# Attention and a GeGLU feed-forward interleaved on one core: down products in one run of 48, gate and up banks read early, maxima of the lead placed earlier

## The chip, the cores and the metric

The kernel runs on one core of a Trainium2 chip. The metric is the device time of one execution in microseconds (us). A comparison of two kernels uses several runs of each; the profile is of one execution. The engines are called TensorE (PE, its weight loads PEld), VectorE (DVE), ScalarE (ACT), GpSimd (POOL) and SyncE (SP, which issues the transfers). L12 is line 12 of the kernel.

## What is computed

```python
xn = layernorm(x)                                  # x: 1 x 2048 x 576
q, k, v = split(xn @ wqkv)                         # 32 heads of 18
p = softmax(q @ k.T * 18 ** -0.5)                  # for each head, 2048 x 2048
s = (p @ v, heads side by side) @ wo
g = silu((gelu(xn @ w_gate) * (xn @ w_up)) @ w_down)   # 576 -> 4608 -> 576, gelu in its tanh form
out = x + s * g
```

All is float32. A factor of a product is split in two parts, high and low (`hi`, `lo`), and a product is made of three: high by high, low by high and high by low.

## The kernel before

A first part (to about 197 us) normalizes x, transposes it, and stores q and k (`qk`), v (`vs`) and the split x (`xhs`) in DRAM. The rest is one long sequence of **144 sections**, each made by `section()` (L422). TensorE runs in the order in which the program is written (`manual_schedule`, L71); on the other engines a scheduler places the instructions, except where `keep_in_program_order` is written.

The feed-forward works on 4 blocks of 512 tokens. A block has 36 sections, each with 128 of the 4608 hidden columns. A section makes 27 *pairs* (`gate_up`, L356): one matmul for gate (`pg`) on the lower 64 rows of the array and one for up (`pu`) on the upper 64, at the same time. Then `activate` (L376) makes gelu(gate) * up in `t1`: ScalarE squares pg (L379), VectorE makes a product with pg (L380), ScalarE takes a tanh (L381), VectorE makes a product with pg (L382) and one with pu (L383). `finish` (L454) splits `t1` into `hh` and `hl`, and after each second section (`G` = 2) it splits the rows of w_down into `dh` and `dl`. `down` (L386) multiplies them: for each of 4 token groups and 2 halves of the columns, 6 matmuls into a bank `py`, which VectorE adds to `Y` (L402; L400 copies in a block's first time). Two sections give 48 such matmuls. `finish` puts them on a list in two halves (24 each, L467 and L468), the first due in the next section and the second in the one after; `downs` (L450) takes from the list what is due.

Attention is woven into this. A *slot* is one part of keys for four heads; it needs maxima (`pm`, `max_mm` L626, read by VectorE at L635) and scores (`pe`, `score_mm` L653, read by ScalarE's exp at L662). Maxima run 40 slots ahead of scores. Sections 0 to 8 are the *lead*: they make maxima only, as many slots as `FIRST` (L41) says. Sections 9 to 136 have 8 slots each: in 16 more pairs a score takes one half of the array and a maximum the other. `spread` (L56) places these special pairs evenly among the 27. After its pairs a section makes the products with v (`values`, L687): 16 groups of matmuls with 32 columns of weights each, four side by side, into `acc` (the profile shows 32 rows for a section). Every fourth section transposes the maxima in between (`max_end`, L641; pm at L644). Sections 132 to 136 have scores only, and 137 to 143 no attention.

After the products with v come, where they are due, the output projection of an earlier block (`project_o`, L523, 15 matmuls into `po`; eight of them for a block, in eight sections one after the other, placed at L564 to L578), and then `downs`. So TensorE's order in a section is: 43 pairs, acc, (pm), (po), 24 py, and the pairs of the next section.

PSUM has 8 banks: tag `f` (2) for pg and pu, `m` (3) for pm and po, `s` (2) for pe and py, and one for acc. So the next section's first pair needs the banks of pg and pu that `activate` of this section reads. When a block is complete, `gates` (L408) takes silu of `Y` in eight pieces (a tanh at L416, two operations on POOL, a store to `ys`); four are done in each of two sections. Key loads (`load_k`, L590, 12 transfers each) and the loads of q (`load_q`, L614) go through SP's queue, as all loads.

The functions that the diff touches follow.

Of the kernel before, what the change touches and what calls it, by code (L numbers as in the profile page):

```python
# [38 lines left out]
NR = F // (G * P)  # L39
NF = NB * NR * G  # L40
FIRST = (0, 3, 5, 5, 5, 5, 5, 6, 6)  # L41
MROW = 3 * DH
HO = 7
KO = HO * DH
# [22 lines left out]
def kernel(ctx: ExitStack, tc: tile.TileContext, x, wqkv, wo, w_gate, w_up, w_down, out):  # L67
# [302 lines left out]

    def gate(o, th, yy):

        nc.scalar.activation(th, yy, AF.Tanh, scale=0.5)
        nc.vector.scalar_tensor_tensor(o, th, 1.0, yy, op0=ALU.add, op1=ALU.mult)

    def activate(pg, pu):  # L376
        t1 = ffn.tile([P, TB], F32, name="t1", bufs=1)
        t2 = ffn.tile([P, TB], F32, name="t2", bufs=1)
        nc.scalar.activation(t1, pg, AF.Square)  # L379
        nc.vector.scalar_tensor_tensor(t2, t1, 1.0 / GC, pg, op0=ALU.add, op1=ALU.mult)  # L380
        nc.scalar.activation(t1, t2, AF.Tanh, scale=GC * GS)  # L381
        nc.vector.scalar_tensor_tensor(t2, t1, 1.0, pg, op0=ALU.add, op1=ALU.mult)  # L382
        nc.vector.scalar_tensor_tensor(t1, t2, 0.5, pu, op0=ALU.mult, op1=ALU.mult)  # L383
        return t1

    def down(b, r, hs, wd, Y, js):  # L386
# [21 lines left out]
    def gates():  # L408

        for k, (b, j, c, Y) in enumerate(FF["gates"]):  # L410
            rows, cc = slice(b * TB + j * P, b * TB + (j + 1) * P), slice(288 * c, 288 * c + 288)
            if k < 3:
                th = op.tile([P, 288], F32, name="th", tag=("yy", "yy", "xx")[k], bufs=(2, 2, 1)[k])
            else:
                th = ffn.tile([P, 288], F32, name="th")
            tc.keep_in_program_order(nc.scalar.activation(th, Y[:, j, cc], AF.Tanh, scale=0.5))  # L416
            nc.gpsimd.tensor_scalar(th, th, 1.0, 1.0, op0=ALU.add, op1=ALU.mult)
            nc.gpsimd.tensor_tensor(th, th, Y[:, j, cc], op=ALU.mult)
            nc.sync.dma_start(ys[rows, cc], th)
        FF["gates"] = []  # L420

    def section(specials=(), tag="f", raw_d=None, early=None):  # L422

        n = FF["n"]
        FF["n"] += 1
        b, r = divmod(n // G, NR)
        g = n % G
        pairs, pg, pu = gate_up(tag)
        if g == 0:
            FF["hs"] = []  # L430
        keep = tc.keep_in_program_order if n == NU * NA + len(FIRST) + 1 else lambda i: i
        nxt = load_gu((n + 1) % (NR * G), keep) if n + 1 < NF else None
        if nxt:
            for k in range(NG - 1):
                split_gu(nxt, k)
        if g == G - 1:
            raw = FF["rawd"] = raw_d() if raw_d else raw_tile([P, G, D])
            nc.sync.dma_start(raw, w_down[r * G * P:(r + 1) * G * P, :].rearrange("(g p) n -> p g n", p=P))
            if early:
                FF["wd"] = early(raw)  # L440
        for p in spread(pairs, specials):
            p()
        if nxt:
            split_gu(nxt, NG - 1)
        FF["w"] = nxt
        if n + 1 < NF and (n + 1) % (NR * G) == 0:
            FF["xd"] = load_xd(b + 1)
        FF["act"] = activate(pg, pu)

    def downs():  # L450
        while FF["down"] and (FF["down"][0][-1] < FF["n"] or FF["n"] == NF):
            down(*FF["down"].pop(0)[:-1])

    def finish(pool=ffn, cut=split, bufs=1):  # L454

        n = FF["n"] - 1
        b, r = divmod(n // G, NR)
        hh = ffn.tile([P, TB], F32R, name="hh", bufs=G + 1)
        hl = ffn.tile([P, TB], F32R, name="hl", bufs=G + 1)
        cut(hh, hl, FF["act"])  # L460
        FF["hs"].append((hh, hl))
        if n % G == G - 1:
            wd = FF.pop("wd", None)
            if not wd:
                wd = [pool.tile([P, G, D], F32R, name=m, bufs=bufs) for m in ("dh", "dl")]
                cut(*wd, FF["rawd"])
            for h in range(2):  # L467
                FF["down"].append((b, r, FF["hs"], wd, FF["Y"], (2 * h, 2 * h + 1), n + 1 + h))  # L468


    op = ctx.enter_context(tc.tile_pool(name="op", bufs=1, reuse_waits="tile"))
# [51 lines left out]
    def project_o(b, i, S2=None, o=None):  # L523
        c, j = divmod(i, TB // P)
        cc = place(b, i)[1]
        if b < NB - 1:
            xx, yy = OG["xy"]
        po = ps.tile([P, TB], F32, name="po", tag="m", bufs=3)
        o = o or OG["o"]
        terms = [(k, x, w) for k in range(NK) for x, w in ((0, 0), (0, 1), (1, 0))]  # L530
        for m, (k, x, w) in enumerate(terms):
            n = min(KO, D - k * KO)
            nc.tensor.matmul(po[:, 0:288], o[x][0:n, k, :], OW[w][0:n, k, :], start=(m == 0), stop=(m == len(terms) - 1))  # L533
        if b < NB - 1:
            nc.vector.scalar_tensor_tensor(yy, yy, 0.5, po[:, 0:288], op0=ALU.mult, op1=ALU.mult)
            nc.gpsimd.tensor_tensor(yy, yy, xx, op=ALU.add)
            OG["y", b, i] = yy
        elif S2 is not None:
            nc.scalar.activation(S2[:, j, cc], po[:, 0:288], AF.Copy)
        return po[:, 0:288]  # L540
# [16 lines left out]
    for b in range(NB):  # L557
        last = b == NB - 1
        for k in range(NK):
            t0 = b * AB + max(-(-min(H, (k + 1) * HO) // QD) * NA + 3, 2 * NA + 10 + 3 * k)  # L560
            if not (last and k == NK - 1):
                at(t0, 0, load_o, b, k)
                at(t0 + 2 - last, 2, norm_o, k)
        first = (b + 1) * AB + 1 if last else max((b + 1) * AB + 6, (b + 1) * NR * G - len(FIRST) + 3)  # L564
        at(first - 2, 0, load_wo, 0)
        at(first - 1, 2, split_o, 0)
        for i in range(GROUPS):
            n = first + i
            if last and n >= ENDS - 1:
                continue  # L570
            if not last:
                at(n, 0, load_xy, b, i)
                at(n + 1, 0, store_y, b, i)
            at(n, 1, lambda b=b, i=i: project_o(b, i, S2[0]))
            if i == TB // P - 1:
                at(n + 1, 0, load_wo, 1)
            if i + 1 < GROUPS:
                at(n, 2, split_o, i + 1)  # L578


    with tc.tile_pool(name="att", bufs=1, reuse_waits="tile") as att:
# [5 lines left out]
        for vv in VS:  # L587
            nc.vector.memset(vv[:, VC * VW:], 0.0)

        def load_k(n, keep=lambda i: i):  # L590

            u, c = divmod(n, NA)
            if u >= NU:
                return
            cols = slice(c * TB, (c + 1) * TB)
            for r in range(2):
                for a in range(2):
                    kk = f(KS[n % KB][r])[64 * a:64 * a + MROW, :]
                    h = QD * (u % NQ) + 2 * r + a
                    rows = slice(D + h * DH, D + (h + 1) * DH)  # L600
                    for n_, i in enumerate((0, 1, 0)):
                        keep(nc.sync.dma_start(kk[n_ * DH:(n_ + 1) * DH, :], qk[i, rows, cols]))
# [8 lines left out]

        QS, MX, ACC, PT, NM, DEN = {}, {}, {}, {}, {}, {}

        def load_q(u):  # L614
            j, g = divmod(u, NQ)
            cols = slice(j * TB, (j + 1) * TB)
            for r in range(2):
                t = QS[u, r] = att.tile([P, TB], F32R, name=f"q{r}", bufs=3)
                for a in range(2):
                    q = f(t)[64 * a:64 * a + MROW, :]  # L620
                    h = QD * g + 2 * r + a
                    rows = slice(h * DH, (h + 1) * DH)
                    for n, i in enumerate((0, 0, 1)):
                        nc.sync.dma_start(q[n * DH:(n + 1) * DH, :], qk[i, rows, cols])
# [101 lines left out]
            t = att.tile([P, QD, TB], F32, name="pT", bufs=4)  # L726
            return t.rearrange("p a t -> p (a t)")[:, 0:G * D].rearrange("p (g d) -> p g d", g=G)

        load_k(0)
        load_q(0)  # L730
        slot, chunk = 0, 1
        for n, m in enumerate(FIRST):
            section([lambda s=s: lead_pair(s) for s in range(slot, slot + m)], "s" if n == 1 else "f", lead_raw)
            slot += m
            while chunk < KB and chunk * SLOTS <= slot + 11:
                load_k(chunk, tc.keep_in_program_order)
# [34 lines left out]
    with tc.tile_pool(name="epi", bufs=1, reuse_waits="tile") as epi:  # L771
# [40 lines left out]
        for Y, j, c in finals:  # L812
            cc = slice(288 * c, 288 * c + 288)
            th = epi.tile([P, 288], F32, name="thl", bufs=len(finals))
            ss = S2[0][:, j, cc]
            gate(th, th, Y[:, j, cc])
            if c * (TB // P) + j > HIND:
                late[c * (TB // P) + j] = th, ss, j, cc
            else:
                nc.vector.scalar_tensor_tensor(ss, th, 0.5, ss, op0=ALU.mult, op1=ALU.mult)  # L820
                put(ss, j, cc, nc.gpsimd)
        for i, o in zip(range(HIND + 1, GROUPS), os):
            th, ss, j, cc = late[i]
            po = project_o(NB - 1, i, o=o)
            nc.vector.scalar_tensor_tensor(ss, th, 0.5, po, op0=ALU.mult, op1=ALU.mult)
            put(ss, j, cc, nc.vector)


# [26 lines left out]
```

## Time and profile before

| what | us |
| --- | --- |
| three runs: lowest, median, highest | 2660.65, 2661.8, 2662.83 |
| the profiled execution: its time | 2661.96 |
| its span, first to last instruction | 2660.2 |
| TensorE busy | 2648.3 |
| VectorE busy | 1991.7 |
| ScalarE busy | 1437.1 |
| GpSimd busy | 1381.0 |

The granted TensorE clock was 1.0 throughout. The lines of the profile name an engine, a line of the kernel, an operation, and what it writes and reads (`acc<-pT,VS`: the tile acc from pT and VS), with partitions x elements. In a timeline the first number is the start in us, the second the duration; what follows in brackets is the engine's idle time just before and what ended it. "x32" says that 32 like instructions in a row are shown as one row. Matmuls overlap, so that durations of neighbours don't add up.

### The profile page before, as it was taken

Reading aid. Unit: us, or ns where it says so; the run is one execution under the profiler, and the core shown is the slowest. Engines: PE = TensorE matmul, PEld = TensorE weight load, DVE = VectorE, ACT = ScalarE, POOL = GpSimd, SP = SyncE. Lnnn points to the kernel's source line nnn. Section 1 sums busy time; section 2 is a strip of 40 time slices with the busy share of each in tenths; the row PEclk is TensorE's granted clock in tenths of the full one; section 3 lists DMA queues with packets and bytes.
Section 4 is the critical chain, followed back from the end, with each engine's and each line's share of the span. In section 5 each row is a group of like instructions: output and inputs, shape, how many; then the busy total and the mean of one; then the engine's idle time right before and its main releaser. Section 6 shows DMA issues by size and latency. Waiting matters only on the chain.

```text
span 2660.2 us, 55706 instructions
## 1 busy us (share of the span) xinstructions
PE 2648.3 (100%) x21064; PEld 2039.8 (77%) x21064; DVE 1991.7 (75%) x3408; ACT 1437.1 (54%) x2553; POOL 1381.0 (52%) x1487
## 2 busy tenths in 40 slices
PE   9999999999999999999999999999999999999999
PEld 8887777777777777777777777777777777777777
DVE  6327888888888877788888877888888777888445
ACT  3222466555666555566556655555666555566532
POOL 2127544544466555554456655554446755544564
PEclk9999999999999999999999999999999999999999
DMA  8865433334354334533346435433345454433342
GB/s 261 264 239 145 111 97 99 94 102 105 103 134 135 96 103 119 138 105 102 99 105 148 121 98 143 121 102 100 100 106 121 131 141 125 115 103 93 76 107 61
DMA packets 390871, 323.64 MB, mean 122 GB/s; under 512 B 105736, under 2 KB 305928, under 8 KB 390604
## 3 DMA queue, kind: packets, MB, share of 16 engines
q1 hardware_dynamic: 390604, 320.08, 44.6%
q8 instruction: 167, 2.74, 0.5%
q14 instruction: 100, 0.82, 0.1%
HBM read 266.58 MB, written 52.85 MB: 120 GB/s over the span
## 4 chain that ended last, share of the span: by engine, by line
PE 97%; DVE 2%; DMA 0%; ACT 0%; issue 0%; SPq 0%; POOL 0%; DVEq 0%; POOLq 0%
PE pg L366 28%; PE py L396 17%; PE acc L695 17%; PE pe L661 10%; PE pm L634 8%; PE po L156 7%; PE pu L366 6%; PE po L533 2%; DVE mx L635 0%; PE po L209 0%; PE pt L218 0%; DVE t L380 0%; DVE Y L402 0%; PE pm L644 0%; DMA pT<-in_B_w_down_dram 0%
## 5 line engine op out<-in xcount | busy, mean ns | idle before, releaser
L662 ACT ACTIVATE pT<-pe 128x512 f32<-128x512 f32 x2048 | 1163.5, 599 | 784.8 <-PE pm L634 614.3
L635 DVE TENSOR_REDUCE mx<-pm 128x1 f32<-128x512 f32 x2048 | 1293.7, 685 | 53.3 <-PE pm L634 31.0
L366 PE MATMUL pg<-xd,wh 64*128 64x512 f32 x2592 | 946.2, 397 | 0.5 <-issue 0.5
L366 PE MATMUL pu<-xd,wh 64*128 64x512 f32 x2592 | 945.8, 397 | 0.1
L661 PE MATMUL pe<-q,KS 56*128 56x512 f32 x2048 | 813.3, 405 | 0.0
L634 PE MATMUL pm<-KS,q 54*128 54x512 f32 x2048 | 797.7, 393 | 2.3 <-DVE mx L635 1.0
L91 POOL TENSOR_SCALAR wh<-raw 128x384 fp32r<-128x384 f32 x432 | 223.1, 517 | 855.3 <-DMA raw<-in_B_w_up_dram 535.0
L366 PEld LDWEIGHTS pg<-xd,wh 64*128 64x128 f32 x2592 | 483.1, 186 | 56.6 <-issue 22.8
L366 PE MATMUL pg<-xd,wl 64*128 64x512 f32 x1296 | 508.3, 392 | 0.0
L366 PE MATMUL pu<-xd,wl 64*128 64x512 f32 x1296 | 508.1, 392 | 0.0
L366 PEld LDWEIGHTS pu<-xd,wh 64*128 64x128 f32 x2592 | 483.7, 187 | 6.7 <-DVE t L383 1.5
L695 PE MATMUL acc<-pT,VS 128*32 128x512 f32 x4096 | 466.0, 595 | 0.0
L92 POOL TENSOR_TENSOR wl<-raw,wh 128x384 fp32r<-128x384 f32 x432 | 437.4, 1013 | 34.5
L661 PEld LDWEIGHTS pe<-q,KS 56*128 56x128 f32 x2048 | 369.5, 184 | 80.9 <-ACT pT L662 22.8
L402 DVE TENSOR_TENSOR Y<-py,Y 128x288 f32<-128x288 f32 x544 | 248.2, 457 | 208.0 <-PE py L396 207.4
L634 PEld LDWEIGHTS pm<-KS,q 54*128 54x128 f32 x2048 | 377.5, 185 | 28.0 <-DVE mx L635 1.9
L396 PE MATMUL py<-dh,hh 128*128 128x288 f32 x1152 | 357.3, 310 | 2.0 <-DVE Y L402 1.0
L396 PE MATMUL py<-dl,hh 128*128 128x288 f32 x1152 | 339.5, 295 | 0.1
L396 PE MATMUL py<-dh,hl 128*128 128x288 f32 x1152 | 338.8, 294 | 0.0
L695 PEld LDWEIGHTS acc<-pT,VS 128*32 128x32 f32 x4096 | 120.5, 109 | 275.5 <-issue 264.3
L396 PEld LDWEIGHTS py<-dh,hh 128*128 128x128 f32 x1152 | 215.9, 187 | 80.7 <-issue 45.3
L366 PEld LDWEIGHTS pg<-xd,wl 64*128 64x128 f32 x1296 | 242.0, 187 | 20.3
(113 smaller groups left out, 2836.1 us busy)
## 6 DMA issues: line engine op xcount, KB each, us to landing
KS<-qk SPq DMA_DIRECT2D x1536, 36.0 KB
raw<-in_B_w_gate_dram SPq DMA_DIRECT2D x144, 288.0 KB
raw<-in_B_w_up_dram SPq DMA_DIRECT2D x144, 288.0 KB
raw<-in_B_w_down_dram SPq DMA_DIRECT2D x68, 576.0 KB
VS<-vs SPq DMA_DIRECT2D x128, 152.0 KB
qk<-t SPq DMA_DIRECT2D x72, 256.0 KB
q<-qk SPq DMA_DIRECT2D x384, 36.0 KB
xd<-xhs SPq DMA_DIRECT2D x24, 384.0 KB
```

The source lines that it names most:

```text
L91: first = nc.gpsimd.tensor_scalar(hi, raw, 1.0, 1.0, op0=ALU.mult, op1=ALU.mult)
L92: nc.gpsimd.tensor_tensor(lo, raw, f(hi), op=ALU.subtract)
L156: nc.tensor.matmul(o, st, m, start=(i == 0), stop=(i == len(TERMS) - 1))
L366: nc.tensor.matmul(o, w[1 + wp][k][rr, c, :], xd[xp][k][rr, c, :], start=(i == 0), stop=(i == len(terms) - 1))
L396: nc.tensor.matmul(py, a[:, tt], w[:, g, cc], start=(n == 0), stop=(n == 3 * G - 1))
L402: nc.vector.tensor_tensor(yy, py, yy, op=ALU.add)
L533: nc.tensor.matmul(po[:, 0:288], o[x][0:n, k, :], OW[w][0:n, k, :], start=(m == 0), stop=(m == len(terms) - 1))
L634: nc.tensor.matmul(pm, QS[u, r][rr, t * P:(t + 1) * P], KS[(u * NA + c) % KB][r][rr, :], start=True, stop=True)
L635: nc.vector.tensor_reduce(MX[u][:, 2 * r + a, t, c:c + 1], pm, axis=AX.X, op=ALU.max)
L661: nc.tensor.matmul(pe, KS[(u * NA + c) % KB][r][rr, t * P:(t + 1) * P], QS[u, r][rr, :], start=True, stop=True)
L662: nc.scalar.activation(PT[u, kt][:, 2 * r + a, :], pe, AF.Exp, scale=SCALE)
L695: nc.tensor.matmul(ACC[u][32 * a:32 * a + 32, :], VS[(u * NA + c) % VB][:, v:v + 32], pt[:, a, :], start=(kt == 0), stop=(kt == NT - 1), s ...
```

## The change

Six things are changed together.

1. `finish` makes both halves of the down products due in the next section, so that 48 run there and none in the section after. Excepted are the sections outside 9 to 136 (`ATT`) and the last pair of sections but one of a block (`r != NR - 2`).
2. `activate` has an early form for sections 9 to 136: ScalarE copies pg to `t2`, VectorE multiplies it by pu, and the last product reads `t1` and `t2` alone. The factor 0.5 is left out of `activate`; the later factors 0.5 become 0.25.
3. `gates` of the first half of a block's `Y` is called between the two halves of the down products; pieces of the second half get the space of `oh` and `ol`.
4. The output projections are placed in every second section, those that have down products; the loads of attention's output start up to four sections later.
5. The first loads of keys and q alternate: keys of rows 0, q of rows 0, keys of rows 1, q of rows 1.
6. In the lead's sections two empty places are added behind the special pairs, so that `spread` puts the maxima nearer to the section's start.

```diff
+ATT = range(len(FIRST), len(FIRST) + NU * NA)
...
-    def activate(pg, pu):
+    def activate(pg, pu, early):
+
         t1 = ffn.tile([P, TB], F32, name="t1", bufs=1)
-        t2 = ffn.tile([P, TB], F32, name="t2", bufs=1)
         nc.scalar.activation(t1, pg, AF.Square)
-        nc.vector.scalar_tensor_tensor(t2, t1, 1.0 / GC, pg, op0=ALU.add, op1=ALU.mult)
-        nc.scalar.activation(t1, t2, AF.Tanh, scale=GC * GS)
-        nc.vector.scalar_tensor_tensor(t2, t1, 1.0, pg, op0=ALU.add, op1=ALU.mult)
-        nc.vector.scalar_tensor_tensor(t1, t2, 0.5, pu, op0=ALU.mult, op1=ALU.mult)
+        nc.vector.scalar_tensor_tensor(t1, t1, 1.0 / GC, pg, op0=ALU.add, op1=ALU.mult)
+        if early:
+            t2 = ffn.tile([P, TB], F32, name="t2", bufs=1)
+            nc.scalar.activation(t2, pg, AF.Copy)
+            nc.vector.tensor_tensor(t2, t2, pu, op=ALU.mult)
+        nc.scalar.activation(t1, t1, AF.Tanh, scale=GC * GS)
+        if early:
+            nc.vector.scalar_tensor_tensor(t1, t1, 1.0, t2, op0=ALU.add, op1=ALU.mult)
+        else:
+            nc.vector.scalar_tensor_tensor(t1, t1, 1.0, pg, op0=ALU.add, op1=ALU.mult)
+            nc.vector.tensor_tensor(t1, t1, pu, op=ALU.mult)
         return t1
...
-            if k < 3:
+            if j >= 2:
+                if c == 0:
+                    free = op.tile([P, NK * P], F32, name="th", tag=("oh", "ol")[j - 2])
+                th = free[:, 288 * c:288 * c + 288]
+            elif k < 3:
...
-            tc.keep_in_program_order(nc.scalar.activation(th, Y[:, j, cc], AF.Tanh, scale=0.5))
+            tc.keep_in_program_order(nc.scalar.activation(th, Y[:, j, cc], AF.Tanh, scale=0.25))
...
     def downs():
         while FF["down"] and (FF["down"][0][-1] < FF["n"] or FF["n"] == NF):
             down(*FF["down"].pop(0)[:-1])
+            if FF["down"] and FF["gates"]:
+                gates()
...
             for h in range(2):
-                FF["down"].append((b, r, FF["hs"], wd, FF["Y"], (2 * h, 2 * h + 1), n + 1 + h))
+                once = n in ATT and n + G in ATT and r != NR - 2
+                FF["down"].append((b, r, FF["hs"], wd, FF["Y"], (2 * h, 2 * h + 1), n + 1 + (0 if once else h)))
...
-            nc.vector.scalar_tensor_tensor(yy, yy, 0.5, po[:, 0:288], op0=ALU.mult, op1=ALU.mult)
+            nc.vector.scalar_tensor_tensor(yy, yy, 0.25, po[:, 0:288], op0=ALU.mult, op1=ALU.mult)
...
-            t0 = b * AB + max(-(-min(H, (k + 1) * HO) // QD) * NA + 3, 2 * NA + 10 + 3 * k)
+            t0 = b * AB + max(-(-min(H, (k + 1) * HO) // QD) * NA + 3, 22 + 3 * k)
...
+        if not last:
+            first += (first + len(FIRST)) % G
...
-            n = first + i
+            n = first + i * (1 if last else G)
...
-        load_k(0)
-        load_q(0)
+        for r in range(2):
+            load_k(0, rs=(r,))
+            load_q(0, (r,))
...
-            section([lambda s=s: lead_pair(s) for s in range(slot, slot + m)], "s" if n == 1 else "f", lead_raw)
+            section([lambda s=s: lead_pair(s) for s in range(slot, slot + m)] + (m > 0) * 2 * [lambda: None],
+                    "s" if n == 1 else "f", lead_raw)
```

The three remaining factors of 0.5 in the last block's gates and in the final products become 0.25 in the same way, and `load_k` and `load_q` take the rows to load as an argument.

More of the change, by code (lines that the diff above doesn't have):

```diff
@@ L371, in gate @@
     def gate(o, th, yy):
-        nc.scalar.activation(th, yy, AF.Tanh, scale=0.5)
+        nc.scalar.activation(th, yy, AF.Tanh, scale=0.25)
         nc.vector.scalar_tensor_tensor(o, th, 1.0, yy, op0=ALU.add, op1=ALU.mult)
-    def activate(pg, pu):
+    def activate(pg, pu, early):
         t1 = ffn.tile([P, TB], F32, name="t1", bufs=1)
-        t2 = ffn.tile([P, TB], F32, name="t2", bufs=1)
         nc.scalar.activation(t1, pg, AF.Square)
[L380 to L383, printed above, removed]
+        nc.vector.scalar_tensor_tensor(t1, t1, 1.0 / GC, pg, op0=ALU.add, op1=ALU.mult)
[9 more added lines that the diff above has]
+            nc.vector.tensor_tensor(t1, t1, pu, op=ALU.mult)
         return t1
@@ L447, in section @@
             FF["xd"] = load_xd(b + 1)
-        FF["act"] = activate(pg, pu)
+        FF["act"] = activate(pg, pu, n in ATT)
     def downs():
@@ L588, with load_k @@
             nc.vector.memset(vv[:, VC * VW:], 0.0)
-        def load_k(n, keep=lambda i: i):
+        def load_k(n, keep=lambda i: i, rs=(0, 1)):
             u, c = divmod(n, NA)
@@ L595, in load_k @@
             cols = slice(c * TB, (c + 1) * TB)
-            for r in range(2):
+            for r in rs:
                 for a in range(2):
@@ L612, with load_q @@
         QS, MX, ACC, PT, NM, DEN = {}, {}, {}, {}, {}, {}
-        def load_q(u):
+        def load_q(u, rs=(0, 1)):
             j, g = divmod(u, NQ)
             cols = slice(j * TB, (j + 1) * TB)
-            for r in range(2):
+            for r in rs:
                 t = QS[u, r] = att.tile([P, TB], F32R, name=f"q{r}", bufs=3)
@@ L819 @@
             else:
-                nc.vector.scalar_tensor_tensor(ss, th, 0.5, ss, op0=ALU.mult, op1=ALU.mult)
+                nc.vector.scalar_tensor_tensor(ss, th, 0.25, ss, op0=ALU.mult, op1=ALU.mult)
                 put(ss, j, cc, nc.gpsimd)
@@ L824 @@
             po = project_o(NB - 1, i, o=o)
-            nc.vector.scalar_tensor_tensor(ss, th, 0.5, po, op0=ALU.mult, op1=ALU.mult)
+            nc.vector.scalar_tensor_tensor(ss, th, 0.25, po, op0=ALU.mult, op1=ALU.mult)
             put(ss, j, cc, nc.vector)
```

## Prediction

> **What bounds the kernel now.** I read the page's first and fourth parts, then the timeline of TensorE, VectorE and ScalarE around two section ends in mid-kernel.
>
> ```profile
> PE 2648.3 (100%) x21064; PEld 2039.8 (77%) x21064; DVE 1991.7 (75%) x3408; ACT 1437.1 (54%) x2553; POOL 1381.0 (52%) x1487
> PE 97%; DVE 2%; DMA 0%; ACT 0%; issue 0%; SPq 0%; POOL 0%; DVEq 0%; POOLq 0%
> PE pg L366 28%; PE py L396 17%; PE acc L695 17%; PE pe L661 10%; PE pm L634 8%; PE po L156 7%; PE pu L366 6%; PE po L533 2%; DVE mx L635 0%; PE po L209 0%; PE pt L218 0%; DVE t L380 0%; DVE Y L402 0%; PE pm L644 0%; DMA pT<-in_B_w_down_dram 0%
> ```
>
> The chain that ended last is TensorE for 97%, and it hardly ever idles: time goes only if TensorE's own row gets shorter, by fewer products, which the change doesn't make, or by cheaper joints between them. So I read the joints. TensorE's timeline from the last pair of section 60 into section 61 (start, duration):
>
> ```profile
> 1210.47 0.39 PE L366 MATMUL pu<-xd,wh 64*128 64x512 f32 x1
> 1210.79 3.64 PE L695 MATMUL acc<-pT,VS 128*32 128x512 f32 x32
> 1214.36 0.40 PE L396 MATMUL py<-dh,hh 128*128 128x288 f32 x1
> 1214.60 0.30 PE L396 MATMUL py<-dl,hh 128*128 128x288 f32 x1
> 1214.73 0.29 PE L396 MATMUL py<-dh,hl 128*128 128x288 f32 x1
> ...
> 1217.54 0.29 PE L396 MATMUL py<-dh,hl 128*128 128x288 f32 x1
> 1217.77 0.50 PE L366 MATMUL pg<-xd,wh 64*128 64x512 f32 x1
> 1217.77 0.50 PE L366 MATMUL pu<-xd,wh 64*128 64x512 f32 x1
> 1218.10 0.40 PE L661 MATMUL pe<-q,KS 56*128 56x512 f32 x1
> ```
>
> Matmuls are pipelined, so differences of starts are the cost, not durations. In a run a py costs 0.13 us, a pair 0.23, a group of four acc 0.43 (the last group starts at 1213.82). At the joints: acc to py 1213.82 to 1214.36 = 0.54, **0.11** more than a group; the first py 0.24, **0.11** more; py to pg 0.22, **0.09** more; the first pair 0.33, **0.10** more. The detour acc, py, pg costs 0.41 in joints, of which 0.20 for leaving acc's shape and re-entering another, twice. The section takes 17.33, and nearly all steady ones do within 0.05 (17.5 where a maximum is transposed, 19.3 with an output projection).
>
> **The change, part by part.**
>
> *48 down products in one run.* In the built order of the instructions 60 sections lose their py altogether and 60 have 48; py to pg joints fall from 141 to 81. A section without py goes from acc (32 times) or from the small transposing product pm of the maxima (28 times) straight to pg. No row shows acc to pg. Upper bound of its extra: what acc to py costs, 0.11, then 0.10 for the first pair, as after py; lower bound: nothing at all, since this row shows a product that follows acc with no extra:
>
> ```profile
> 1195.41 1.46 PE L695 MATMUL acc<-pT,VS 128*32 128x512 f32 x11
> 1196.70 0.38 PE L644 MATMUL pm<-ident,nm 128*16 128x128 f32 x2
> 1197.01 0.40 PE L396 MATMUL py<-dh,hh 128*128 128x288 f32 x1
> ```
>
> pm starts 0.43 after the last acc group, its weights were loaded beneath acc; but py behind pm then waits again (0.20 after pm's second pass, 0.09 too many), so the pm sections have the same 0.4 before and would keep 0.2. I take the dearer end, because pg has 128 columns of weights as py has and pm only 16: 0.41 - 0.21 = 0.195 saved, 60 x 0.195 = **-11.7 us**; with nothing left of the joint it is 60 x 0.41 = -24.6; if the straight joint were as dear as the detour, 0. The Trainium skill, "TensorEngine Tiling (Array Packing)", section Tiling Modes, says that a change of tiling mode drains TensorE. By that rule acc to pg pays as acc to py does and the sum is the -11.7; pm behind acc, 0.00 extra, shows that not every change of shape pays, and by that row it would be -24.6.
>
> Eight py in a row instead of four need no more than two banks: one py bank takes 0.79 to fill, VectorE's eviction 0.46, and it idles 0.34 between two of them in the rows of L402.
>
> *gate and up banks freed early.* In a section without py only acc's 3.57 us stand between the last pair and the next pg, which needs the same two banks. ScalarE and VectorE at that place, before:
>
> ```profile
> 1211.16 0.59 ACT L379 ACTIVATE t<-pg 128x512 f32<-128x512 f32 x1
> 1212.51 0.63 ACT L381 ACTIVATE t<-t 128x512 f32<-128x512 f32 x1 [0.75 <-DVE t L380]
> 1214.55 0.60 ACT L700 ACTIVATE accs<-acc 128x512 f32<-128x512 f32 x1 [1.41 <-PE acc L695]
> ```
>
> ```profile
> 1211.78 0.69 DVE L380 SCALAR_TENSOR_TENSOR t<-t,pg 128x512 f32<-128x512 f32 x1 [0.31 <-ACT t L379]
> 1213.17 0.69 DVE L382 SCALAR_TENSOR_TENSOR t<-t,pg 128x512 f32<-128x512 f32 x1 [0.70 <-ACT t L381]
> 1213.99 0.69 DVE L383 SCALAR_TENSOR_TENSOR t<-t,pu 128x512 f32<-128x512 f32 x1
> 1218.57 0.69 DVE L635 TENSOR_REDUCE mx<-pm 128x1 f32<-128x512 f32 x1 [0.24 <-PE pm L634]
> ```
>
> The old chain lets pu go at 1214.68; without py the next pg starts at 1213.82 + 0.54 = 1214.36: 0.32 late. The new chain: Square, L380's product to 1212.47, then ScalarE's copy of pg (as built it waits for that product) at the price of L700, a copy out of the same kind of bank, 0.60, then t2 x pu at L383's 0.69, with 0.04 at each hand-over: pu is free at 1213.85, **0.5 early**. Queued behind the copy are the tanh (ends 1213.8) and the next exps, which aren't due before 1215.1 (0.77 after pg, as 1218.54 is here); behind the last product on VectorE (ends 1214.6; with the two small casts of a maximum, 0.28 each, 1215.2) is the next maximum, due at 1215.15 to 1215.35. So the new work costs **0** while acc covers it. All 123 sections with maxima have the same times here within 0.02. In sections 133 and 135 there are no maxima, ScalarE's exps end 0.5 later, and 0.13 is missing: **+0.3**.
>
> *gates, projections, loads.* A block's silu begins a section earlier, in the run of 48, behind its section's tanh; four tanh at 0.43 are through before the next exps. On SP its four stores go in front of four key loads; keys are issued 11 us or more ahead of use around block ends, 16 elsewhere, so they stay covered. POOL's splits of w_gate and w_up stand 12 us or more ahead, those of w_down 8.4 (3.7 at block ends, where the change keeps two runs of 24): the shorter section takes at most 3.3 us of that. The projections go to every second section and sit in front of py there as now: 0. The factor 0.25 for 0.5 costs nothing.
>
> *lead's maxima ahead.* The lead's sections 1 to 8 (204 to 298 us) do have stalls:
>
> ```profile
> 206.81 0.47 PE L634 MATMUL pm<-KS,q 54*128 54x512 f32 x1 [0.71 <-issue]
> 207.88 0.47 PE L634 MATMUL pm<-KS,q 54*128 54x512 f32 x1 [0.60 <-DMA q<-qk]
> 249.48 0.49 PE L366 MATMUL pg<-xd,wh 64*128 64x512 f32 x1
> 249.90 0.49 PE L366 MATMUL pu<-xd,wh 64*128 64x512 f32 x1
> ```
>
> In section 1 the first slot waits 2 us for q. The new order of loads brings its q earlier, but the second slot's q stays the last of the 24 loads (issued to 208.4, here landing some 1.9 later, at about 210.0), and that slot moves from pair 17 to pair 10: TensorE stands there till 210.0 and then has 17 pairs and a slot left, to 214.3, where it was through at 212.86: **+1.4**. Section 2's first py waited 0.4 for dl, which is then ready: **-0.4**. Later, each section loses 0.4 on pu (249.48 to 249.90) and 0.3 to 0.4 among py to VectorE; with its maxima done, the chain starts up to 0.3 earlier: -0.2 in some five sections, **-1.0**. Against it, the slots are now 1.1 us apart (1.0 with six), and VectorE needs 2 x 0.61 for each (nine in 5.75): **+0.15** in five sections, **+0.3** in the two of six: +1.3. Sum of the lead: **+1.3**, bounds -3 and +4.
>
> **Sum:** -11.7 + 0.3 + 1.3 = -10.1 on the profiled execution's 2661.96 (span 2660.2 and 1.8 around it), 2651.9; the median shown is 0.2 lower: **2651.7**.
>
> **Rivals.**
> *The joint vanishes* (pg's weights load beneath acc as pm's do): -24.6 + 1.6, **2639**. For it: pm. Against: every row that enters 128 columns pays.
> *Nothing is saved*: the straight joint costs the detour's 0.41: 2661.8 + 1.6, **2663**. Against: the extras sit one at each change of shape, and one change is gone.
> *The lead loses its whole bound* of 4 with the joints as forecast: **2654.4**.
> *Slower: pu comes free too late.* If copy and product end 0.82 or more later than reckoned (as when pu were let go only after tanh and the last product, or ScalarE's exps ran over as in 133), each of 60 sections stalls 0.32, as with the old chain: +19.2 - 10.1, **2670.9**. It takes effect beyond 0.5 of delay and turns the sign beyond 0.67. Against: fixed rows, and as built pu's bank waits for t2 x pu alone.
>
> **How the numbers follow.** Forecast 0.68 (its own range 2648 to 2656), lead's bound 0.06, joint vanishes 0.08, nothing saved 0.10, pu late 0.08. The range 2641 to 2656.5 takes in the first two and part of the third. A measurement here can tell about 0.2%, 5.3 us, from no change. Faster: 0.68 + 0.06 + 0.08 = 0.82; same 0.10; slower 0.08.
>
> **What would show it.** Sections alternating at 13.9 (14.1 with pm) and 20.5 us; acc to pg near 0.54 and the first pair 0.33; pg and pu of a section behind no py starting together (apart: pu late); ScalarE's copy 0.6; section 1 ending near 214. I am wrong if acc to pg is 0.43 or 0.7, or if pu waits.

## The result, and the profile after

| what | before | after |
| --- | --- | --- |
| runs, side by side | 18 | 18 |
| median, us | 2661.72 | 2656.35 |
| lowest to highest, us | 2660.26 to 2663.66 | 2653.42 to 2659.01 |
| profiled execution: time, span | 2661.96, 2660.2 | 2655.02, 2653.2 |

The ratio of the times is 0.998, with a 95% interval of 0.9973 to 0.9987: 5.4 us less, where the prediction had 10.1 less. The median lies 0.15 us inside the upper end of the prediction's range (2656.5) and outside the 2648 to 2656 that it gave to its own forecast. The page of the changed kernel, parts 1 and 4:

```profile
PE 2641.2 (100%) x21064; PEld 2038.2 (77%) x21064; DVE 1996.9 (75%) x3408; ACT 1500.3 (57%) x2681; POOL 1389.4 (52%) x1487
PE 97%; DVE 2%; ACT 1%; POOL 0%; SPq 0%; issue 0%; DMA 0%; DVEq 0%; POOLq 0%; ACTq 0%
```

TensorE is still the whole chain, with the same 21064 matmuls in 7.1 us less; ScalarE has 128 instructions more, the copies. The joints, from the end of section 61 (no py) in TensorE's timeline, and from the end of section 64 (48 py):

```profile
1227.89 3.64 PE L712 MATMUL acc<-pT,VS 128*32 128x512 f32 x32
1231.46 0.50 PE L367 MATMUL pg<-xd,wh 64*128 64x512 f32 x1
1231.47 0.50 PE L367 MATMUL pu<-xd,wh 64*128 64x512 f32 x1
1231.80 0.39 PE L678 MATMUL pe<-q,KS 56*128 56x512 f32 x1
```

```profile
1278.45 3.64 PE L712 MATMUL acc<-pT,VS 128*32 128x512 f32 x32
1282.02 0.40 PE L404 MATMUL py<-dh,hh 128*128 128x288 f32 x1
1282.26 0.30 PE L404 MATMUL py<-dl,hh 128*128 128x288 f32 x1
...
1288.44 0.29 PE L404 MATMUL py<-dh,hl 128*128 128x288 f32 x1
1288.66 0.50 PE L367 MATMUL pg<-xd,wh 64*128 64x512 f32 x1
1289.00 0.40 PE L678 MATMUL pe<-q,KS 56*128 56x512 f32 x1
```

pg starts 3.57 us after the first acc, and so does py: the straight joint has the price of acc to py (0.52 behind the last matmul of acc, in all 32 places), and the first pair takes 0.33 in both. pg and pu start together, so pu's bank was free. ScalarE and VectorE ahead of that joint of section 61:

```profile
1228.26 0.59 ACT L380 ACTIVATE t<-pg 128x512 f32<-128x512 f32 x1
1229.61 0.60 ACT L384 ACTIVATE t<-pg 128x512 f32<-128x512 f32 x1 [0.75 <-DVE t L381]
```

```profile
1228.89 0.69 DVE L381 SCALAR_TENSOR_TENSOR t<-t,pg 128x512 f32<-128x512 f32 x1 [0.31 <-ACT t L380]
1230.24 0.69 DVE L385 TENSOR_TENSOR t<-t,pu 128x512 f32<-128x512 f32 x1 [0.66 <-ACT t L384]
```

pu is let go at 1230.93, 0.53 ahead of pg.

Where the 6.9 us of the two profiled spans come from, by the starts of the sections in both traces: +0.3 ahead of section 0, +0.9 in sections 0 to 8, -9.1 in the sections 9 to 131 apart from one wait, +0.8 for that wait (section 38), +0.2 behind section 131.

Two places lose. In section 1 the second slot of maxima waits for q and for keys, twice:

```profile
208.22 0.47 PE L651 MATMUL pm<-KS,q 54*128 54x512 f32 x1 [1.07 <-DMA q<-qk]
209.55 0.47 PE L651 MATMUL pm<-KS,q 54*128 54x512 f32 x1 [0.86 <-DMA KS<-qk]
```

And section 38 takes 21.36 us where other sections of 48 py without a projection take 20.57. Its down products stop in the middle of the run; TensorE, ScalarE and GpSimd there:

```profile
817.69 0.40 PE L404 MATMUL py<-dh,hh 128*128 128x288 f32 x1 [0.54 <-DVE Y L408]
```

```profile
813.80 0.60 ACT L380 ACTIVATE t<-pg 128x512 f32<-128x512 f32 x1 [1.60 <-POOL hl L93]
```

```profile
800.71 1.28 POOL L504 TENSOR_TENSOR OT<-OT,den 126x512 f32<-126x512 f32 x1 [4.43 <-DMA den<-rT]
...
807.12 0.83 POOL L429 TENSOR_SCALAR th<-th 128x288 f32<-128x288 f32 x2
807.91 1.57 POOL L430 TENSOR_TENSOR th<-th,Y 128x288 f32<-128x288 f32 x2
809.45 0.83 POOL L429 TENSOR_SCALAR th<-th 128x288 f32<-128x288 f32 x2
810.24 1.57 POOL L430 TENSOR_TENSOR th<-th,Y 128x288 f32<-128x288 f32 x2
811.78 0.62 POOL L92 TENSOR_SCALAR hh<-t 128x512 fp32r<-128x512 f32 x1
812.48 1.28 POOL L93 TENSOR_TENSOR hl<-t,hh 128x512 fp32r<-128x512 f32 x1
```

Read from the bottom up. GpSimd stood 4.43 us for the transfer of den, then made L504, three splits of weights, eight operations of the gates (4.8 us) and only then the split of section 37's gelu. `t1` has one buffer, so section 38's square (L380) waits for this split, 1.60 us; behind it the whole gelu is late, and VectorE's copies of py into Y (L408) are queued behind the gelu.

### The profile page after: what moved, and what is told of

Same layout as the page of the kernel before. It is cut to its first block, busy times and chain, and to the rows that moved or that the text cites. A ratio compares the mean times of both kernels' runs of the same rounds, so it can differ in the third digit from the quotient of the medians.

```text
span 2653.2 us, 56039 instructions
## 1 busy us (share of the span) xinstructions
PE 2641.2 (100%) x21064; PEld 2038.2 (77%) x21064; DVE 1996.9 (75%) x3408; ACT 1500.3 (57%) x2681; POOL 1389.4 (52%) x1487
## 4 chain that ended last, share of the span: by engine, by line
PE 97%; DVE 2%; ACT 1%; POOL 0%; SPq 0%; issue 0%; DMA 0%; DVEq 0%; POOLq 0%; ACTq 0%
PE pg L367 28%; PE py L404 17%; PE acc L712 17%; PE pe L678 9%; PE pm L651 9%; PE po L157 7%; PE pu L367 7%; PE po L548 2%; PE po L210 0%; PE pt L219 0%; DVE mx L652 0%; PE pm L661 0%; DVE t L381 0%; DVE Y L410 0%; ACT t L380 0%
## 5 line engine op out<-in xcount | busy, mean ns | idle before, releaser
L93 POOL TENSOR_TENSOR wl<-raw,wh 128x384 fp32r<-128x384 f32 x432 | 438.6, 1016 | 34.3
L367 PEld LDWEIGHTS pg<-xd,wl 64*128 64x128 f32 x1296 | 242.0, 187 | 20.6
```

Source lines behind the costliest of these rows:

```text
L93: nc.gpsimd.tensor_tensor(lo, raw, f(hi), op=ALU.subtract)
L367: nc.tensor.matmul(o, w[1 + wp][k][rr, c, :], xd[xp][k][rr, c, :], start=(i == 0), stop=(i == len(terms) - 1))
```

## The experiments

Each kernel is compared with the kernel before, run beside it; differences below are against that. The changed kernel stands at -5.4.

| kernel | ratio, 95% interval | us against before |
| --- | --- | --- |
| the change | 0.998, 0.9973 to 0.9987 | -5.4 |
| e1_old_lead | 0.9971, 0.9959 to 0.9982 | -7.2 |
| e2_pu_late | 1.0037, 1.0024 to 1.0051 | +9.8 |
| e3_two_halves | 1.0013, 1.0004 to 1.0022 | +3.6 |
| e4_po_odd | 1.0002, 0.9993 to 1.0011 | +0.8 |
| e5_old_loads | 0.998, 0.9971 to 0.9989 | -5.3 |
| e6_old_places | 0.9972, 0.9961 to 0.9983 | -7.1 |
| e7_all_once | 1.0055, 1.0042 to 1.0068 | +15.0 |
| e8_norm_later | 0.9966, 0.9953 to 0.9979 | -8.5 |
| e10_gates_once | 0.9978, 0.9969 to 0.9987 | -5.4 |
| e11_gates_behind | 0.9965, 0.9952 to 0.9977 | -9.4 |

Differences of 1 or 2 us between two of these are within the intervals; where they carry a verdict, lengths of sections in the traces have to carry it with them, and where these don't, the text says so.

### The joints: e3_two_halves, e4_po_odd

```diff
-once = n in ATT and n + G in ATT and r != NR - 2
-FF["down"].append((b, r, FF["hs"], wd, FF["Y"], (2 * h, 2 * h + 1), n + 1 + (0 if once else h)))
+FF["down"].append((b, r, FF["hs"], wd, FF["Y"], (2 * h, 2 * h + 1), n + 1 + h))
```

> Part 1 is undone: the down products are due in two halves of 24 in two sections, as before; all else of the change stays. My theory: the joints are the gain, 0.157 us for each section by the sections' lengths after (a pair of sections 34.50 instead of 34.66), so 58 to 60 sections give back 9.1 to 9.4, and the time is about 2665.5, which is before's 2661.7 plus the change's costs (lead 0.9, section 38's wait 0.8, and what else it has). Rival: part of the gain comes from elsewhere (gates earlier, projections, early banks): between 2657 and 2663.

It is 9.0 us slower than the change, and slower than before. So the gain is the run of 48, and without it the rest of the change costs 3.6 (in its profile 2.5 in sections 0 to 8 and 1.7 in sections 9 to 131).

```diff
-first += (first + len(FIRST)) % G
+first += 1 - (first + len(FIRST)) % G
```

> The output projections of the first three blocks (24 in all) are put into the sections that have no down products; all else of the change stays. My theory: in such a section TensorE then goes from acc to po and from po to the gate product, so the detour of joints that the change takes away is paid again, 24 x 0.16 to 0.20 = 4 to 4.7 us, about 2660.7. Rival: it is the number of down products in a run, not the joints, that counts: then the projections cost the same wherever they stand, and the time is 2656.4. Second rival: VectorE's or ScalarE's work behind po delays the banks of the next section, more than 5 us.

6.1 us slower than the change. At the end of section 61, where a projection now stands alone:

```profile
1235.34 1.04 PE L712 MATMUL acc<-pT,VS 128*32 128x512 f32 x8
1236.31 0.40 PE L548 MATMUL po<-woh,oh 126*128 126x288 f32 x1
1236.55 0.29 PE L548 MATMUL po<-wol,oh 126*128 126x288 f32 x1
...
1238.27 0.29 PE L548 MATMUL po<-woh,ol 72*128 72x288 f32 x1
1238.49 0.50 PE L367 MATMUL pg<-xd,wh 64*128 64x512 f32 x1
```

The first po takes 0.24, po to pg 0.22, as py did. From the last acc to the next pg such a section has 2.702 us (median of 12), one without anything 0.522; ahead of a run of py a projection costs 1.980 (9.140 against 7.160). So a projection alone costs 0.20 more, 24 of them 4.8: the joint, paid by another product. The other 1.3 us have no place of their own. In this profile, whose execution is the longest of the eleven, the stretch of pairs is 0.025 us longer than in the change's in each of the 123 sections, 3 us in all. It is longer than before, by 0.01 to 0.03, in the other experiments as well (mean 10.373 to 10.395, leaving out the kernels that wait there; 10.366 before, 10.370 in the change's); its cause stays open. pg and pu start together in all 24 sections, so the second rival is out.

### The early banks: e2_pu_late

```diff
-FF["act"] = activate(pg, pu, n in ATT)
+FF["act"] = activate(pg, pu, False)
```

> Part 2 is undone: everywhere the late form of the gelu, in which VectorE's last product reads the up bank behind the tanh. The rest stays. My theory, as in the prediction: the bank comes free 0.32 us after it is due in 60 sections, so that 0.32 x 60 = 19 us are lost, about 2675, slower than before; the up product of a section behind no py starts some 0.3 us after its gate product. Rival: the early form was not needed, since the scheduler or the clocks of the engines leave slack: 2656, the same as the change.

15.2 us slower than the change. TensorE and VectorE at the end of section 65:

```profile
1311.35 0.49 PE L367 MATMUL pg<-xd,wh 64*128 64x512 f32 x1
1311.69 0.49 PE L367 MATMUL pu<-xd,wh 64*128 64x512 f32 x1
```

```profile
1310.95 0.69 DVE L391 TENSOR_TENSOR t<-t,pu 128x512 f32<-128x512 f32 x1
```

pu waits for the last product, 0.34 behind pg: the 0.32 of the prediction. Behind a pm it waits only 0.13 to 0.14, since the transposing product gives the banks 0.20 more; of the 60 places 30 have 0.33 to 0.35, 27 have 0.13 to 0.15, one has 0.49, and the two behind sections 133 and 135, which have no maxima, have 0.70: 15.7 us in all, not 19.

### The lead: e1_old_lead, e5_old_loads, e6_old_places

```diff
-for r in range(2):
-    load_k(0, rs=(r,))
-    load_q(0, (r,))
+load_k(0)
+load_q(0)
...
-    section([lambda s=s: lead_pair(s) for s in range(slot, slot + m)] + (m > 0) * 2 * [lambda: None],
-            "s" if n == 1 else "f", lead_raw)
+    section([lambda s=s: lead_pair(s) for s in range(slot, slot + m)], "s" if n == 1 else "f", lead_raw)
```

> Parts 5 and 6 of the change are undone (order of the first loads, places of the lead's maxima); the rest stays. My theory, from the changed kernel's sections: the lead costs, its sections 0 to 8 take 0.91 us more than before, section 1 alone 0.6. Without it the span is about 0.9 us shorter and the median about 2655.4. If the wait of the second slot for q is also what scatters the changed kernel's runs (2653.4 to 2659.0, where the kernel before has 2660.3 to 2663.7), the runs lie as close together as those of the kernel before. Rival: the lead's earlier maxima pay for themselves further on, and without them the time is the same or 0.5 longer; the scatter stays as wide.

e5 has the first half of this edit, e6 the second.

> Part 5 alone is undone: the first loads are all keys and then all q, as before; the lead's maxima keep their earlier places (part 6). My theory: what costs in the lead is that the second slot of section 1 now stands at pair 10 and waits for the last load whatever the order of the loads; and as q of rows 0 now comes later, the first slot waits too. Section 1 then takes 9.4 to 12.3 us, as in the profiles with both parts, and the time is as the change's, 2656 to 2657 (0.998 of before). Rival: the new order of loads is at fault: section 1 falls to about 8 and the time to that of the kernel with both undone (0.997).

> Part 6 alone is undone: the lead's maxima stand as before, the first loads alternate (part 5). My theory: the second slot of section 1 stands at pair 17 again, and its wait for the last load is covered by pairs: section 1 takes 7.6 to 8.8 us or less, sections 7 and 8 lose no 0.3 and 0.8 to VectorE's maxima, and the time is 1.8 below the change's or a little better, ratio to before 0.9971 or 0.997. Rival: the order of loads costs by itself: as slow as the change, 0.998.

By the medians undoing the places gives 1.8 us, with either order of loads (-7.2 and -7.1 against -5.4 and -5.3), and the loads give nothing. The intervals overlap, so look at the sections. Section 1 took 9.4, 10.9, 11.9, 12.3 and 10.8 us in the five profiles with the new places, and 7.4 to 8.8 in the seven with the old ones. In e1 TensorE waits once in that section, for 0.48 us, and no longer for the second slot:

```profile
206.63 0.47 PE L651 MATMUL pm<-KS,q 54*128 54x512 f32 x1 [0.48 <-DMA q<-qk]
208.81 0.59 PE L651 MATMUL pm<-KS,q 54*128 54x512 f32 x2
```

The waits alone don't make the long sections 1. In e5 TensorE idles 1.58 us there, in the change's profile 1.93, and yet e5's section is 1.4 us longer. The difference is the granted clock, here in the same stretch of e5 and of the change's profile:

```profile
208.50:211.90 3.40, 3.36 (x18) 0.50 0.36 101
```

```profile
208.50:211.90 3.40, 2.54 (x21) 1.00 0.37 105
```

Behind the stretch and its length stand TensorE's busy time, the number of its matmuls and the clock (0.50 and 1.00). For 3.4 us behind the waits e5 had half the clock, a pair took 0.43 us instead of 0.23, and that costs 1.7 us. Without the idle time section 1 takes 7.15 to 7.47 us in the eight profiles without this and 9.05 to 9.2 in the four with it: e2, e3, e4 and e5. So all four other profiles with the new places have it, and the change's own, with 1.93 us of waits, has not; what decides isn't shown.

The old places are no safeguard. In e6's profile sections 0 to 8 took 2.2 us more than before, more than the change's 0.9: section 2 is 15.96 us long instead of 12.9, since a maximum waited for VectorE, which stood behind the gelu of section 1, and then the clock was 0.5 for 3.4 us there:

```profile
218.08 0.49 PE L651 MATMUL pm<-KS,q 54*128 54x512 f32 x1 [2.67 <-DVE mx L652]
```

This execution is the longest of e6's eight. So the 1.8 us rest on the medians and on section 1, and the places are not the only cause of a long lead.

The expectation on the scatter is not borne out: e6 has the old places, and its eight runs still lie 2651.2 to 2656.7. The clock goes with the scatter. Of the change's 18 runs the five with a mean granted clock of 1.0 have a median of 2654.4, the other 13 (0.998 or 0.999) one of 2656.6; in e3 and in e5 the five runs with 1.0 are the five shortest of eleven. A single run can't be sorted by this mean, since the last few us of an execution, at half clock too, move it as much.

### The ends of the blocks: e7_all_once, e8_norm_later, e10_gates_once, e11_gates_behind

These four have parts 5 and 6 undone, so their base is e1 (-7.2); e10 and e11 have the edit of e8 as well. e7:

```diff
-once = n in ATT and n + G in ATT and r != NR - 2
+once = n in ATT and n + G in ATT
```

> On the kernel with parts 5 and 6 undone: the exception for the last pair of sections but one of a block is taken out, so that 48 down products stand in one run there too (sections 34, 70 and 106) and three more sections have none. My theory: each run saves its section's 0.157 us of joints, three of them 0.5 in all, no more than can be told, and sections 34 and 35 together go from 35.0 to 34.8. Rival: the block's end is tight, since the splits of w_gate, w_up and x for the new block and the gates need POOL just there: a wait of some us in one of the sections 35 to 38, 71 to 74 or 107 to 110, and the time is 1 to 5 us longer.

The rival holds, and far beyond its price: 22 us slower than e1. Sections 36, 72 and 108, the first of a block, take 28.8, 29.9 and 26.9 us instead of 20.6. One of several waits of up products there, and GpSimd ahead of them:

```profile
769.31 0.50 PE L367 MATMUL pu<-xd,wh 64*128 64x512 f32 x1 [0.92 <-POOL xd L127]
```

```profile
761.64 1.46 POOL L127 CAST xd<-xd 64x1536 fp32r<-64x1536 f32 x1 [6.07 <-DMA xd<-xhs]
```

The new block's x (`xd`) isn't there. With section 35 only 14 us long its loads come too late: SyncE stood 10.6 us at a weight load for a buffer that GpSimd had not yet split, with the loads of xd queued behind. TensorE idles 5.1, 4.8 and 3.3 us in these three sections, and the granted clock was 0.5 there for 3.4, 6.8 and 3.4 us, which costs up to 6.8 us more. The one exception in the change's list of runs is worth 22 us.

e8 holds GpSimd's L504 at its place, behind the gates:

```diff
-nc.gpsimd.tensor_tensor(OT[0:n, k, :], OT[0:n, k, :], den[0:n], op=ALU.mult)
+tc.keep_in_program_order(nc.gpsimd.tensor_tensor(OT[0:n, k, :], OT[0:n, k, :], den[0:n], op=ALU.mult))
```

> On the kernel with parts 5 and 6 undone: GpSimd's product of attention's output with the reciprocals (L504) is held at its place in the program, behind the gates of section 38, where the scheduler had put it ahead of them, and so GpSimd stood 4.4 us for the transfer of den. My theory: this wait made the splits and the gates late, then the gelu of section 37 and Y's additions in section 38, whose down products waited 0.8 us in the changed kernel's profile and 0.3 in that with the old lead. Without it section 38 takes 20.57 as other sections of 48 and the time is 0.3 to 0.8 us less (as much as can hardly be told; the section tells it). Rival: the wait in section 38 has another cause, the gates themselves between the two halves: section 38 stays at 20.9 to 21.4.

Section 38 took 20.57. But section 74 took 20.84, and section 110 took 21.74, after a wait of GpSimd for a part of w_up (3.64 us, until 2080.92) ahead of the same eight operations. GpSimd idles 3.4 to 4.8 us at all three block ends in all profiles with 48 py there, for one thing or another. So the theory was too narrow: what counts is when it resumes, and how much then stands in front of the split: the eight operations, and in section 38 the 1.28 of L504 as well. e10 undoes part 3, so that all eight pieces fall into one section:

```diff
 down(*FF["down"].pop(0)[:-1])
-if FF["down"] and FF["gates"]:
-    gates()
```

> On the kernel with parts 5 and 6 undone and L504 held at its place: part 3 is undone, so that all eight pieces of a block's gates come in section 37 (73, 109) and none in the section before. My theory: section 37 is the short one, without down products; GpSimd has 16 operations, 9.6 us, ahead of the split of section 37's gelu instead of 8 with 4.8 us; so this split comes up to 4.8 us later, the gelu of section 38 with it, and Y's additions in sections 38, 74 and 110 make the down products wait, 1 to 4.8 us each, 3 to 14 in all. Rival: what the first four pieces leave free in section 36 is idle time of GpSimd, the splits fit behind the eight, and nothing is lost: 2652, the same.

3.1 us slower than e8; sections 38, 74 and 110 take 21.4, 21.4 and 22.5. But most of it is not GpSimd's. ScalarE and TensorE at the start of section 38:

```profile
798.66 2.77 ACT L428 ACTIVATE th<-Y 128x288 f32<-128x288 f32 x8
801.33 2.94 ACT L677 ACTIVATE pT<-pe 128x512 f32<-128x512 f32 x5
```

```profile
801.96 0.50 PE L676 MATMUL pe<-q,KS 56*128 56x512 f32 x1 [0.56 <-ACT pT L677]
```

Eight tanh, 2.77 us, run over into section 38, and the scores wait for the exps behind them, 0.86 us in each of the three; only in section 110 does the expected wait of the down products come on top (1.05). Four tanh end in time, as forecast.

e11 leaves the tanh and writes GpSimd's half of these pieces behind the split, held there:

```diff
+later = []
-gates()
+gates(later)
...
 finish()
+for rest in later:
+    rest()
```

> On the same kernel: the GpSimd half of the second four pieces of the gates is written behind the split of section 37's gelu and held there, so that only three of their eight operations (1.6 instead of 4.8 us) come ahead of the low part of that split; the tanh stay. My theory: the waits in sections 38, 74 and 110 that come and go with GpSimd's transfers (0.3 to 1.2 us, mostly one section in an execution) are gone, all three take 20.57 to 20.61, the median is 0.3 to 1 us less than with L504 held alone (ratio to before 0.9962 to 0.9966) and the runs lie closer together. Rival: with the pieces behind, Y or the splits of the next section are late instead, and some of the sections 38 to 40 are longer.

GpSimd in section 38 of this kernel:

```profile
803.01 0.44 POOL L430 TENSOR_SCALAR th<-th 128x288 f32<-128x288 f32 x1
803.53 0.81 POOL L431 TENSOR_TENSOR th<-th,Y 128x288 f32<-128x288 f32 x1
804.31 0.43 POOL L430 TENSOR_SCALAR th<-th 128x288 f32<-128x288 f32 x1
804.71 0.62 POOL L92 TENSOR_SCALAR hh<-t 128x512 fp32r<-128x512 f32 x1
805.29 0.81 POOL L431 TENSOR_TENSOR th<-th,Y 128x288 f32<-128x288 f32 x1
806.06 1.29 POOL L93 TENSOR_TENSOR hl<-t,hh 128x512 fp32r<-128x512 f32 x1
```

Four of the eight (2.5 us; not three, as expected) are ahead of the low part of the split now. It ends at 807.35, 1.9 us before the square is due. The fair comparison is section 74 of e1, where GpSimd resumed 2.11 us into the section, the split ended at 11.91 and the section took 20.85: here it resumed at 2.17, and the split ended at 9.66. Sections 38, 74 and 110 take 20.57, 20.57 and 20.54. The median, 2651.82, is the best of all, 9.4 under before and 4 under the change; against e8 the 0.9 us are within the intervals.

With all profiles together the mechanism has a number. Undisturbed, the square of these three sections starts 10.73 us into the section. In the kernels with 48 py there (e2 and e10 aside, whose py start later) the run of py stopped by what the square was later than 11.65:

| square at | section | length beyond 20.57 |
| --- | --- | --- |
| 11.58 | e8, 38 | 0.00 |
| 11.69 | e6, 38 | 0.04 |
| 11.97 | e1, 38 | 0.30 |
| 12.28 | e5, 38 | 0.61 |
| 12.45 | the change, 38 | 0.79 |
| 12.83 | e8, 110 | 1.17 |

The other sections 38, 74 and 110 of these profiles fit within 0.03. The cover is 0.9 us, and what lies beyond is paid in full.

## Why the prediction was right, and where its size was off

**The forecast's mechanism** came out: the straight joint costs one change of shape, the detour two. "Joint vanishes" and "nothing saved" are out (0.52, not 0.43 or 0.7; e3). The Trainium skill, "TensorEngine Tiling (Array Packing)", section Tiling Modes, says that a change of tiling mode drains TensorE. The trace agrees for acc to pg, acc to py and acc to po, which all take 0.52; acc to the small pm takes 0.41, and whether that is a change of mode no run here shows.

**The step that failed in size is the first term of the sum**, "0.41 - 0.21 = 0.195 saved, 60 x 0.195 = -11.7". Measured are -9.1 in sections 9 to 131: two sections without pm and po take 34.50 instead of 34.66, 58 such pairs, 0.157 each. Between the last acc and the next pg a section of 24 py had 3.923 us: 0.523, the first py 0.237, 22 more 2.944 (0.1338 each), py to pg 0.220. One of 48 has 7.160, in which the 24 added py take 3.235, or 0.1348 each. So the run that was taken away cost 0.237 + 2.944 + 0.220 = 3.401 and comes back at 3.235: 0.166. The two joints of a run, reckoned with 0.1338 for a py, are 0.189, so that calling a py 0.13 made only 0.006 of the error. 0.024 is what the 24 added py lose again, and it sits where a bank is used anew. VectorE's addition that empties a bank, and TensorE's weight load and matmuls behind it:

```profile
1283.12 0.46 DVE L410 TENSOR_TENSOR Y<-py,Y 128x288 f32<-128x288 f32 x1 [0.83 <-PE py L404]
```

```profile
1283.63 0.19 PEld L404 LDWEIGHTS py<-dh,hh 128*128 128x128 f32 x1
```

```profile
1283.72 0.31 PE L404 MATMUL py<-dh,hh 128*128 128x288 f32 x1
1283.87 0.30 PE L404 MATMUL py<-dl,hh 128*128 128x288 f32 x1
```

From the third bank of a run on, the weight load of a bank's first py comes 0.054 us after the end of that addition (before, in the change and in e11, with one exception), and on average 0.16 to 0.175 behind the load before it, where the others take 0.133. So it waits for VectorE, and the bank's second py starts 0.14 to 0.155 after its first instead of 0.133. A run of 24 has two such places and a run of 48 six. "No more than two banks", priced at nothing, thus cost some 0.02 for each run. From 0.166 to 0.157 it is the stretches of pairs, 0.004 longer each. A thing repeated 60 times and worth 0.2 wants its rows in nanoseconds.

**The gate and up banks freed early** were right, to 0.03: copy 0.60, product 0.69, pu free 0.53 ahead (0.5 forecast). Behind sections 133 and 135 pu is 0.10 late, 0.2 in all (0.3 forecast). The slower rival's point held as well, and only its price was off: 15.7 instead of 19, since a pm covers 0.20 of a wait, which the prediction had in its own rows.

**The gates, costed at nothing,** were not free. I asked whether the splits of the weights stay ahead (12 us) and whether four tanh fit (they do; eight don't, e10), but not what stands behind the gates on GpSimd: the split of a gelu, on which the next square hangs with 0.9 us of cover. It cost 0.8 us in the profiled execution, and 0.6 to 1.4 in those of e1, e4, e5, e6 and e8.

**The lead** was right in place and sign: section 1 stood for its second slot until 209.55 (210.0 forecast) and ended at 213.8 (214). The profiled execution lost 0.9 (1.3 forecast), but that they are so close is luck: section 1 cost 0.6 instead of 1.4, the 0.4 foreseen for section 2 didn't come (12.93 against 12.91), and it was a lucky execution: in the other four profiles with the new places section 1 was 1.4 to 2.9 us longer. Each of them has the half clock behind the waits, 1.7 us, for which the prediction has no term. By the medians the places cost 1.8. The gain foreseen in later sections was there (sections 3, 5 and 6 are 0.2 to 0.35 shorter) and less than what sections 7 and 8 lose (0.3 and 0.75, forecast 0.3 each).

**Sum** for the profiled execution: -9.1 for the joints, +0.9 lead, +0.8 block end, +0.3 ahead of section 0 (not in the change), +0.2 behind section 131 (the last two pairs of sections save 0.3 there, pu costs 0.2 and section 136 another 0.3): -6.9. The medians differ by 5.4 only. Of the 1.5 between them 1.3 is the profiled execution's own place, below the median of its kernel; the 3.4 us at half clock, which it escaped, are worth 1.7 in an execution that has them. That the median lies within the range at all, by 0.15 us, is luck: the joints gave 2.6 less than forecast, and neither the half clock nor the block ends were reckoned with. What else scatters the runs, the lengths of the pairs among it, stays open.

## What to carry to other kernels

On a TensorE that never idles look for changes of shape: two runs of the same products put together save the entry and the exit of one, here 0.166 us each time, if something frees the banks that the run was covering. When you move work on an in-order engine, ask of it not only what it waits for but what waits behind it: eight short operations ahead of one split were harmless until GpSimd came to them a microsecond later. And look at the granted clock in every profile: a place that makes TensorE wait for a transfer can cost, in some executions, 1.7 us more than the wait, and one profile doesn't show it.

## What the runs showed of the hardware

The product of t1 and t2 (L388) is new in that both operands lie in SBUF, and its duration depends on GpSimd. VectorE and GpSimd in the changed kernel, at the end of section 37, where GpSimd's L504, shown above, runs from 800.71 for 1.28 us:

```profile
800.91 1.63 DVE L388 SCALAR_TENSOR_TENSOR t<-t,t 128x512 f32<-128x512 f32 x1
```

```profile
801.97 0.95 POOL L92 TENSOR_SCALAR wh<-raw 128x384 fp32r<-128x384 f32 x1
```

L388 ends 0.55 us after L504. (So it does in section 10, where GpSimd's L93 ends at 330.65 and L388 at 331.20.) Of its 128 instances 99 start with no GpSimd operation under way and take 0.691 to 0.694; the 26 that start during a TENSOR_TENSOR have a median of 1.03 and reach 1.68. GpSimd pays as well: the TENSOR_SCALAR above takes 0.95 instead of 0.51. The products that read one operand from PSUM (L381, L385) never exceed 0.691, of which 101 start during a TENSOR_TENSOR. The other profiles with this product have it too, and e2, which has no such product, has none over 0.690 in its last product (L391). The Trainium skill, "SBUF — State Buffer", section Who interferes with whom, states it: VectorE with two SBUF inputs and a reading GpSimd operation exclude each other. The trace agrees. I had priced L388 as the old product with PSUM, 0.69. One place in the change's profile paid for it: in section 136 L388 took 1.45 us, VectorE's next addition to Y came late, and the run of py lost 0.34. Elsewhere no wait of TensorE was traced to it; no experiment of its own was made.
